# Block-sparse attention with a soft mixture of experts: the turned probabilities of a tile share one buffer, and neighbouring keys share products

## The chip, the cores and the metric

The kernel runs on one core of one Trainium2 chip. The metric is the device time of one launch in microseconds (us), the median of the runs shown.

## The reference

Four batches of eight heads, 768 positions, 64 values a head; positions are grouped into 24 blocks of 32. A query block sees its own block and the two beside it, the first and the last block (the "boundary" blocks), and three sampled blocks; the first and last query blocks see everything. The attention's output (3072 x 512) goes through a soft mixture of 8 experts with 4 slots each.

```python
mask = np.abs(blk_i - blk_j) <= 1
mask = mask | (blk_i == 0) | (blk_j == 0) | (blk_i == n_blocks - 1) | (blk_j == n_blocks - 1)
for qb in range(n_blocks):
    for kb in sampled_blocks[qb]:
        mask[qb*32:(qb+1)*32, kb*32:(kb+1)*32] = True
attn = softmax(np.where(mask, q @ k.T / 8, -1e9))
x = (attn @ v)                       # as 3072 x 512
logits = x @ phi                     # 512 x 32 slots
d = softmax(logits, axis=0); c = softmax(logits, axis=1)
slot_input = d.T @ x
slot_out[e] = np.maximum(slot_input[e] @ w1[e], 0) @ w2[e]
out = c @ slot_out
```

## The kernel before

All of the arithmetic is in float32. The kernel has three stages: attention with the logits of the mixture beside it, the experts, and the output.

In attention the 22 inner query blocks of a batch are taken in 11 *pairs*. For a pair, `stage_k` (L414) gathers for each of its two blocks the 256 keys that it sees into a buffer `kst`, eight blocks of 32: three neighbours, two boundary blocks, three sampled ones. The fixed blocks are copied by POOL (L434, L436), the sampled ones by ACT (L442) or POOL (L444). `qk` (L515) makes the scores `s`, VectorE their maxima `nm` (L530), ACT the probabilities `p` (L535), and VectorE turns them by transposes of 32 x 32 into `ptt` (L542), so that keys lie on the partitions. The 128 partitions of a turned tile are four heads of 32 keys, and there are two such sets of heads, r = 0 and 1. `stage_v` (L460) gathers the values of the sampled blocks into `vrs`.

Two neighbouring pairs make a *full tile* of four query blocks, 128 output rows; there are five in each batch, and one tile of a single pair beside the dense first and last blocks. `av_heads` multiplies the turned probabilities with the values (`v`, and `vrs` for the sampled blocks) into the PSUM tile `av`, of which there is one; all of its products stand on one line, L593 (`av_mm`). A product's stationary side is a part of `ptt`: 64 partitions (two heads, the index g) by as many columns as query rows take part, 32 for each block; its moving side is 130 columns of values. Two r passes fill a full tile. Then VectorE normalizes into `x` (L587 to L589), TensorE transposes `x` (`mxt`, L772), and four tiles form a group for the logits (`ml`), their running sums (`ms`) and `d`; there are six groups. The dense blocks have their own scores (`sd`, L684) and products (`avd`, also L593).

The order on each engine is written once, at build time, by a planner (`Plan.run`): every step is a task with the steps that it needs, a key, a cost that its author put in (2.36 for one r pass of a full tile), and the buffers that it takes from named rings (`ptt` 4, `x` 6, `s` 4, `av` 1). The planner goes through the tasks by their earliest start and lists the instructions of each engine in that order. SP's loads of the expert weights are paced by TensorE's progress, into buffers that are kept for them or that attention has given back.

The layout of `ptt` before: for each tile and r a buffer of eight slots by four query blocks by 32, the slots being the eight key blocks of each query's own list. Slots 4 and 5 hold the boundary blocks for all four query blocks. A neighbour that two blocks of one pair share stands in the same slot for both (slots 1 and 2), so their product has 64 columns; the other neighbours and the sampled ones are products of 32 columns.

Of the kernel before, what the change touches and what calls it, by code (L numbers as in the profile page):

```python
# [11 lines left out]
F32 = mybir.dt.float32  # L12
I32 = mybir.dt.int32
# [22 lines left out]


NKST, NVR, NQ = 4, 6, 4
PB, PTB, XB, XTB = 4, 4, 6, 4
SB, MB = 4, 2  # L40

LD0, LD1 = 3, 12
# [140 lines left out]
def attn_moe_kernel(ctx, tc, qT, kT, vfull, vtab, sampled, phi, w1, w2, out):  # L183
# [64 lines left out]
    ssum = const.tile([P, 1], F32, name="ssum")  # L248


    sreg = const.tile([1, NB, NR], I32, name="sreg")

    vreg = const.tile([1, NB, NR], I32, name="vreg")

    scr = pw.tile([P, DM], F32, tag="x", name="scr", bufs=XB)

# [44 lines left out]
        n = (B * (NB - 2) + n) % NVR  # L301
        vrs[n] = pst.tile([P, 2, NR, 2 * D1], F32, name=f"vrs{n}")

    nq = [0]

    def load_q(b, g, eng=None):
        q = qst[nq[0] % NQ]
# [43 lines left out]
    def evac(out, in_, eng):  # L351
        if eng in ("A", "ACT"):
            ACT.copy(out=out, in_=in_)  # L353
        else:
            DVE.tensor_copy(out=out, in_=in_)

    plan = Plan(tc, dict(s=SB, av=1, pt=MB, p=PB, ptt=PTB, kst=NKST, vrs=NVR, x=XB, xT=XTB, k=2, v=2, q=NQ,
                     ptd=1, lp=1, dT=1, d=1), free=("pt",))
    add = plan.add

    class Rec:
# [15 lines left out]
    use = []  # L377
    t_warm = add(warm, ("PE", 4.0), [], -41, acq=[("s", use)])
    use.append(t_warm)
    t_sreg = add(sreg_copy, ("DVE", 0.3), [t_idx], -39)  # L380
    t_vreg = add(lambda t: index_math(), ("DVE", 4.0), [t_sreg], -38)

# [37 lines left out]

    fresh, nst, nvs = {}, [0], [0]

    def stage_k(b, i, n, use):
        k = nst[0] % NKST
        nst[0] += 1
        st, new = kst[k], fresh.get(k) != b
        fresh[k] = b

        w, r0 = (0, 96) if i % 2 else (32, 0)

        def fixed(t):
            kv = ktile[b]
            if new:
                POOL.tensor_copy(out=st[:, :, 128:192].rearrange("p c (g s) -> p c g s", g=2),  # L434
                                 in_=kv.rearrange("p c (g s) -> p c g s", g=NB)[:, :, 0:NB:NB - 1, :])
            POOL.tensor_copy(out=st[:, :, w:w + 96], in_=kv[:, :, (i - 1) * BLK:(i + 2) * BLK])  # L436

        def sampled_(t):
            for j, o in enumerate((r0, 192, 224)):
                src = ktile[b][:, :, ds(t.vals[j] * BLK, BLK)]  # L440
                if t.eng == "ACT":
                    ACT.activation(out=st[:, :, o:o + BLK], in_=src, func=AF.Copy, scale=1.0)  # L442
                else:
                    POOL.tensor_copy(out=st[:, :, o:o + BLK], in_=src)  # L444

        f = add(fixed, ("POOL", 0.82 if new else 0.47), [t_k[b]], n - 4, acq=[("kst", use)])
        r = add(sampled_, [("ACT", 0.62), ("POOL", 0.73)], [f, t_sreg], n - 2.5,
                pre=lambda e: block_numbers(sreg, i, e, NB - 1))
        k_use[b].extend([f, r])
        use.extend([f, r])  # L450
        return st, r
# [43 lines left out]

    def plan_pair(b, g, n):
        T = tile_of(b, (g + 1) // 2)
        w = 1 if g and g % 2 == 0 else 0
        u = Rec()
        u.g = g  # L500
        kd, ku = [], []
# [20 lines left out]
            use.append(t_qk)  # L522
        u.p = [None] * 2
        if not T.turned:
            T.pt = [None] * 2
        for r in range(2):
            def top(t, r=r):
                u.nm = getattr(u, "nm", {})
                u.nm[r] = pw.tile([P, 2], F32, tag="nm", name="nm", bufs=4)
                DVE.tensor_reduce(out=u.nm[r], in_=u.s[r], axis=AX.X, op=ALU.max, negate=True)  # L530

            def exp(t, r, j):
                if j == 0:
                    u.p[r] = pw.tile([P, 2, 256], F32, tag="p", name="p", bufs=PB)
                ACT.activation(out=u.p[r][:, j, :], in_=u.s[r][:, j, :], func=AF.Exp,  # L535
                               bias=u.nm[r][:, j:j + 1], scale=1.0)


            def turn(t, r=r):
                if w == 0:  # L540
                    T.pt[r] = pw.tile([P, 8, 4, BLK], F32, tag="ptt", name="ptt", bufs=PTB)
                DVE.transpose(out=T.pt[r][:, :, 2 * w:2 * w + 2, :].rearrange("p k j q -> p j k q"),  # L542
                              in_=u.p[r].rearrange("p j (k q) -> p j k q", k=8))

            t_m = add(top, ("DVE", 0.6), [t_qk], n + 0.1 + 0.01 * r)
            p_use = []
            t_e = []
            for j in range(2):
                t_e.append(add(lambda t, r=r, j=j, exp=exp: exp(t, r, j), ("ACT", 0.37), [t_m] + t_e, n + 0.2 + 0.01 * r,
                               acq=[("p", p_use)] if j == 0 else []))  # L550
            s_use[r].append(t_e[1])
            acq = []
            if w == 0:
                T.pt_use = getattr(T, "pt_use", {})
                T.pt_use[r] = []
                acq = [("ptt", T.pt_use[r])]
            t_t = add(turn, ("DVE", 0.64), [t_e[1]] + ([T.turned[r]] if w else []), n + 0.3 + 0.01 * r, acq=acq)
            p_use.append(t_t)
            T.turned.append(t_t)
# [41 lines left out]
    def av_heads(T, rs_):  # L601

        vt, us = vtile[T.b], T.units
        one = len(us) == 1
        m = 64 * len(us)
        for n, c in enumerate((4, 5)):
            for r in rs_:
                for g, s_ in G2:
                    av_mm(T.av, 64 * r if one else 0, m, g, r, T.pt[r][s_, c, 0:m // BLK].rearrange("p j q -> p (j q)"),
                          vt[s_, :, VPOS((0, NB - 1)[n]), r, :], n == 0, False)  # L610
        for c in (1, 2):
            for w, u in enumerate(us):
                for r in rs_:
                    for g, s_ in G2:
                        av_mm(T.av, 64 * r if one else 64 * w, 64, g, r,
                              T.pt[r][s_, c, 2 * w:2 * w + 2].rearrange("p j q -> p (j q)"),
                              vt[s_, :, VPOS(2 * u.g + c), r, :], False, False)
        for n in range(NR + 1):
            for w, u in enumerate(us):
                for r in rs_:  # L620
                    for j in range(2):
                        i = 2 * u.g + 1 + j
                        for g, s_ in G2:
                            if n == 0:

                                k, c = (i - 1, 0) if j == 0 else (i + 1, 3)
                                if k in (0, NB - 1):
                                    continue
                                v_ = vt[s_, :, VPOS(k), r, :]
                            else:  # L630
                                c = ((3, 0)[j], 6, 7)[n - 1]
                                v_ = u.vst[j][s_, :, n - 1, r, :]
                            av_mm(T.av, (64 * r if one else 64 * w) + 32 * j, 32, g, r, T.pt[r][s_, c, 2 * w + j], v_,
                                  False, n == NR)

    def plan_av(T, n):
        deps = T.turned + T.staged + [t_v[T.b]]
        use, x_use = [], T.x_use
        if len(T.units) == 1:
            def both(t):  # L640
                new_av(T)
                av_heads(T, range(2))

            def out(t):
                for r in range(2):
                    av_out(T, T.av, 64 * r, 64 * r + 64, slice(r, r + 1), 0)
            t_a = add(both, ("PE", 2.45), deps, n + 0.5, acq=[("av", use)])
            T.out = [add(out, ("DVE", 1.68), [t_a], n + 0.6)]
        else:
            def heads(t, r):  # L650
                if r == 0:
                    new_av(T)
                av_heads(T, (r,))
            t_0 = add(lambda t: heads(t, 0), ("PE", 2.36), deps, n + 0.5, acq=[("av", use)])
            t_a = add(lambda t: heads(t, 1), ("PE", 2.36), [t_0], n + 0.5)
            T.out = [add(lambda t: av_out(T, T.av, 0, P), ("DVE", 1.06), [t_a], n + 0.6, acq=[("x", x_use)])]
        x_use.extend(T.out)
        use.extend(T.out)
# [106 lines left out]
    def plan_group(gi, Ts, last, final=False):  # L765
# [65 lines left out]
            PE.transpose(st.pd, st.dT, ident)  # L831

        def dout(t):
            st.d = pw.tile([P, P], F32, tag="d", name="d", bufs=1)
            evac(st.d, st.pd, "D")

        def sums(t):
# [25 lines left out]
        lp_use.extend([t_lt, t_e])  # L863
        t_dt = add(dturn, ("PE", 0.25), [t_e], k + 0.4, acq=[("pt", use[2])])
        dT_use.append(t_dt)
        t_do = add(dout, ("DVE", 0.2), [t_dt], k + 0.5, acq=[("d", d_use)])
        use[2].append(t_do)
        t_s = add(sums, ("PE", 1.1), [t_do], k + 0.6, acq=[("pt", use[3])])
        d_use.append(t_s)
# [60 lines left out]
    def c_out(g, bank, eng="A"):  # L930
        if g in (3, 4):
            cT[g] = pw.tile([P, 4, P], F32R, tag="p", name="cT", bufs=PB)
        elif g in (0, 2):
            both_ = pw.tile([P, 2, 4, P], F32R, tag="ptt", name="cT", bufs=PTB)
            cT[g], cT[{0: 1, 2: 5}[g]] = both_[:, 0], both_[:, 1]
        evac(cT[g], bank, eng)

    def plan_combine(g, n, dep=[]):
# [123 lines left out]
    for j, g in enumerate((0, 1, 2, 5)):  # L1062
# [8 lines left out]
        t_n = add(lambda t, g=g: c_rest(g), ("POOL", 0.95), [t_n], n + 0.1)  # L1071
        t_n = add(turn, ("PE", 0.62), [t_n, done[-1][1].t_av], n + 0.2, acq=[("s", b_use)])
        p_use.append(t_n)
        b_use.append(add(lambda t, g=g: c_out(g, cb[g]), ("ACT", 0.6), [t_n], n + 0.3, acq=[("ptt", [])] if g in (0, 2) else []))
    c3 = plan_combine(3, k + 1.2, [t_7])
    t_8 = add(lambda t: c_max(4), ("DVE", 0.55), [t_lst[m] for m in range(16, 20)] + [t_7], k + 1.7)
    add(lambda t: c_exp(4), ("ACT", 0.32), [t_8], k + 1.8)
# [286 lines left out]
```

## Time and profile before

| | |
|---|---|
| median of three runs | 314.02 us (312.48 to 316.74) |
| profiled execution | 318.06 us, its span 316.3 us |
| TensorE busy | 281.0 us, 89% of the span |
| VectorE, POOL, ACT busy | 214.8, 181.1, 164.7 us |
| HBM read, written | 56.19 MB, 6.29 MB |
| probability products (L593, `av`) | 1728 records with `v`, 2112 with `vrs` |

A float32 product leaves two records of TensorE (PE) in the trace, and two weight loads (PEld). In a row, "64*128 64x130" is a product with 64 partitions by 128 output rows on the stationary side and 130 moving columns on 64 partitions. Page part 2 shows TensorE near full from the first microseconds to the end of the expert stage, and the DMA engines at nine tenths or more in the last quarter of the span.

### The profile page before, as it was taken

The numbers are of one execution on the slowest core, as the hardware profiler recorded it, in microseconds if no ns is written. First come the engines' busy times: TensorE is split into PE (matmuls) and PEld (weight loads), VectorE is DVE, ScalarE is ACT, GpSimd is POOL, SyncE is SP. The second block draws the span as 40 slices with busy tenths as digits, with TensorE's granted clock in tenths as the row PEclk, the third lists the DMA queues.
The fourth block names the chain that finished last, engine by engine and source line by source line (L and its number), as shares of the span: only waits on it lengthen the run. The fifth ranks groups of instructions, "written<-read, shape, count | busy, mean of one in ns | idle before, by whom it ended". The sixth has DMA issues, their size and how long they took to land.

```text
span 316.3 us, 17629 instructions
## 1 busy us (share of the span) xinstructions
PE 281.0 (89%) x7179; PEld 193.9 (61%) x7179; DVE 214.8 (68%) x495; ACT 164.7 (52%) x505; POOL 181.1 (57%) x503
## 2 busy tenths in 40 slices
PE   7499789799997989999999999997997999999960
PEld 7148557466774656778676667864765774355540
DVE  4799766658997589789977878997597335012260
ACT  0856665853666687636757753764662140102350
POOL 2879488685954868776688885748557314000000
PEclk9999999999999999999999999998999999999996
DMA  7935777610265725034575311668688999999998
GB/s 250 398 103 173 218 204 208 165 41 3 71 184 153 206 75 146 6 87 138 138 219 139 115 55 34 167 187 222 183 226 271 367 302 370 368 412 407 393 356 288
DMA packets 34227, 63.63 MB, mean 201 GB/s; under 512 B 5601, under 2 KB 19042, under 8 KB 34146
## 3 DMA queue, kind: packets, MB, share of 16 engines
q1 hardware_dynamic: 34000, 62.37, 61.9%
q8 instruction: 57, 0.93, 1.3%
q14 instruction: 24, 0.20, 0.2%
q10 hardware_dynamic: 146, 0.13, 0.1%
HBM read 56.19 MB, written 6.29 MB: 198 GB/s over the span
## 4 chain that ended last, share of the span: by engine, by line
PE 56%; DMA 14%; DVE 9%; issue 7%; POOL 3%; ACT 3%; POOLq 3%; ACTq 2%; SPq 1%; DVEq 0%
PE av L593 24%; PE s L515 7%; DMA q<-in_qT_dram 6%; PE pf L1162 4%; PE avd L593 4%; DMA w<-in_w_dram 3%; PE sd L684 3%; PE mxt L772 3%; PE pso L1170 3%; DMA v<-in_vfull_dram 3%; POOLq L341 2%; PE ml L790 2%; DMA ktile<-in_kT_dram 2%; DVE ptt L542 2%; ACTq L341 2%
## 5 line engine op out<-in xcount | busy, mean ns | idle before, releaser
L460 POOL COPY vrs<-v 128x260 f32 x264 | 96.0, 407 | 31.9 <-PE av L593 22.3
L535 ACT ACTIVATE p<-s,nm 128x256 f32<-128x256 f32 x176 | 72.2, 476 | 15.4 <-DVE nm L530 12.9
L593 PE MATMUL av<-v,ptt 64*64 64x130 f32 (+2 forms) x1728 | 75.8, 287 | 0.4 <-issue 0.4
L542 DVE STREAM_TRANSPOSE ptt<-p 128x512 f32<-128x512 f32 x88 | 58.8, 693 | 21.2 <-ACT p L535 21.1
L593 PEld LDWEIGHTS av<-v,ptt 64*64 64x64 f32 (+2 forms) x1728 | 50.9, 133 | 27.7 <-issue 18.0
L515 PE MATMUL s<-kst,q 64*32 64x256 f32 x1408 | 53.5, 382 | 10.5 <-ACT p L535 6.0
L530 DVE TENSOR_REDUCE nm<-s 128x2 f32<-128x512 f32 x88 | 55.4, 671 | 0.5 <-PE s L515 0.3
L436 POOL COPY kst<-ktile 128x384 f32<-128x384 f32 x88 | 42.9, 509 | 14.6 <-PE s L515 12.2
L593 PE MATMUL av<-vrs,ptt 64*32 64x130 f32 x2112 | 46.5, 275 | 4.3 <-issue 4.2
L442 ACT ACTIVATE kst<-ktile 128x128 f32 x174 | 39.5, 305 | 11.3 <-PE s L515 8.3
L515 PEld LDWEIGHTS s<-kst,q 64*32 64x32 f32 x1408 | 28.9, 106 | 23.6 <-ACT p L535 9.4
L593 PEld LDWEIGHTS av<-vrs,ptt 64*32 64x32 f32 x2112 | 35.3, 105 | 7.0 <-issue 6.2
L593 PE MATMUL avd<-v,ptd 64*64 64x130 f32 x768 | 23.8, 271 | 0.7 <-DVE ptd L719 0.4
L353 ACT COPY xT<-mxt 128x512 f32<-128x512 f32 x20 | 11.7, 585 | 24.4 <-PE mxt L772 23.0
L715 ACT ACTIVATE pd<-sd,nb 128x384 f32<-128x384 f32 x32 | 16.6, 577 | 14.8 <-DVE nb L710 14.3
L593 PEld LDWEIGHTS avd<-v,ptd 64*64 64x64 f32 x768 | 22.0, 132 | 3.0 <-PE s L515 1.5
L444 POOL COPY kst<-ktile 128x128 f32 x90 | 22.7, 296 | 1.0 <-issue 0.6
L477 ACT ACTIVATE q<-q 128x256 f32<-128x256 f32 x26 | 10.8, 417 | 19.0 <-DMA q<-in_qT_dram 18.7
L479 POOL TENSOR_SCALAR q<-q 128x256 f32<-128x256 f32 x22 | 8.9, 407 | 17.3 <-DMA q<-in_qT_dram 17.3
L772 PE MATMUL mxt<-ident,x 128*128 128x128 f32 x96 | 15.8, 286 | 3.2 <-DVE x L589 3.2
L772 PEld LDWEIGHTS mxt<-ident,x 128*128 128x128 f32 x96 | 10.1, 141 | 13.7 <-DVE x L589 6.0
L587 DVE TENSOR_SCALAR rs<-av 128x8 f32<-128x8 f32 (+1 forms) x28 | 4.5, 162 | 20.6 <-PE av L593 20.4
(117 smaller groups left out, 296.8 us busy)
## 6 DMA issues: line engine op xcount, KB each, us to landing
q<-in_qT_dram SPq DMA_DIRECT2D x47, 128.0 KB, 2.7
w<-in_w_dram SPq DMA_DIRECT2D x44, 128.0 KB, 3.0
w<-in_w_dram SPq DMA_DIRECT2D x11, 512.0 KB, 9.6
out_dram<-ob SPq DMA_DIRECT2D x22, 256.0 KB, 4.3
ktile<-in_kT_dram SPq DMA_DIRECT2D x48, 96.0 KB, 2.9
w<-in_w_dram SPq DMA_DIRECT2D x18, 256.0 KB, 6.6
v<-in_w_dram SPq DMA_DIRECT2D x24, 128.0 KB, 3.4
v<-in_w_dram SPq DMA_DIRECT2D x12, 256.0 KB, 5.3
```

Of the source, the lines that this page charges most:

```text
L341: _, vals = nc.values_load_multi_w_load_instructions(t[0:1, i, :], engines=[{"ACT": E_.Activation, "POOL": E_.Pool}[eng]], min_val=0, max_ ...
L436: POOL.tensor_copy(out=st[:, :, w:w + 96], in_=kv[:, :, (i - 1) * BLK:(i + 2) * BLK])
L442: ACT.activation(out=st[:, :, o:o + BLK], in_=src, func=AF.Copy, scale=1.0)
L444: POOL.tensor_copy(out=st[:, :, o:o + BLK], in_=src)
L460: POOL.tensor_copy(out=st[:, :, j:j + 1, :], in_=vf[:, :, ds(t.vals[j], 1), :])
L515: PE.matmul(u.s[r][32 * p:32 * p + 32, j, :], lhsT=u.q[s_, p, j, :], rhs=kd[j][0][s_, p, :], start=True, stop=True)
L530: DVE.tensor_reduce(out=u.nm[r], in_=u.s[r], axis=AX.X, op=ALU.max, negate=True)
L535: ACT.activation(out=u.p[r][:, j, :], in_=u.s[r][:, j, :], func=AF.Exp, bias=u.nm[r][:, j:j + 1], scale=1.0)
L542: DVE.transpose(out=T.pt[r][:, :, 2 * w:2 * w + 2, :].rearrange("p k j q -> p j k q"), in_=u.p[r].rearrange("p j (k q) -> p j k q", k=8))
L593: PE.matmul(av[o:o + m, g, r * 2 * D1:(r + 1) * 2 * D1].rearrange("p (a d) -> p a d", a=2), lhsT=lhsT, rhs=rhs, start=start, stop=stop)
L715: ACT.activation(out=u.p[r][k], in_=u.s[r][k], func=AF.Exp, bias=u.nb[r], scale=1.0)
L772: PE.transpose(T.px[:, c, :], T.x[:, c * P:(c + 1) * P], ident)
```

## The change

The four `ptt` buffers become one, with four places of eleven slots that begin nine slots apart. Query block c of a tile (c = 0 to 3) lies c slots further than before, and the order of the keys in `kst` now depends on c, so that a key block that several query blocks of the tile see as a neighbour stands in one slot for all of them. The slots of the tile: 3 and 4 are the boundary blocks, 5 to 10 the neighbours, and the sampled blocks take what is left. Each neighbouring key block is then one product for the query blocks from `lo` to `hi`: one, two, three or four of them. For the third one, the range is widened to all four blocks, and the place of the first block, which doesn't see this key, holds zeros, which POOL writes once at the start. The boundary products stay as they were (128 columns), and so do the 24 sampled ones of a pass (32 columns). Per pass of a full tile there are 40 products for 44. For tiles of a single pair the products have the same widths as before.

To make room, `x` has five buffers for six, `d` shares the buffer of `lp`, and `sreg` and `vreg` share one. The cost of a pass in the planner becomes 2.15.

```diff
-PB, PTB, XB, XTB = 4, 4, 6, 4
+PB, PTB, XB, XTB = 4, 4, 5, 4
+PTS, PTD = 11, 9
...
+    ptt = pw.tile([P, (PTB - 1) * PTD + PTS, 4, BLK], F32, name="ptt", tag="ptt", bufs=1)
...
+    def zeros(t):
+        for r in range(PTB):
+            POOL.memset(ptt[:, PTD * r + 8, 0, :], 0.0)
...
+    SPOS = [[k for k in range(5) if k not in (3 - c, 4 - c)] for c in range(4)]
...
-        w, r0 = (0, 96) if i % 2 else (32, 0)
+        c = (i + 1) % 4
+        w, o_ = 5 * BLK, (3 - c) * BLK
...
-            T.pt = [None] * 2
+            T.pt = [ptt[:, PTD * ((nt[0] + r) % PTB):PTD * ((nt[0] + r) % PTB) + PTS] for r in range(2)]
+            nt[0] += 2
...
-                if w == 0:
-                    T.pt[r] = pw.tile([P, 8, 4, BLK], F32, tag="ptt", name="ptt", bufs=PTB)
-                DVE.transpose(out=T.pt[r][:, :, 2 * w:2 * w + 2, :].rearrange("p k j q -> p j k q"),
-                              in_=u.p[r].rearrange("p j (k q) -> p j k q", k=8))
+                a_ = T.pt[r][:, 2 * wl, 2 * wl, :].copy()
+                o = bass.AP(a_.tensor, a_.offset, [list(a_.ap[0]), [5 * BLK, 2], [4 * BLK, 8], [1, BLK]])
+                DVE.transpose(out=o, in_=u.p[r].rearrange("p j (k q) -> p j k q", k=8))
...
-        for c in (1, 2):
-            for w, u in enumerate(us):
+        for s in (1, 2, 3, 4, 0, 5):
+            k = k0 + s - 1
+            lo, hi = max(c0, (0, 0, 0, 0, 2, 3)[s]), min(4, s + 1)
+            if lo < hi and k not in (0, NB - 1):
                 for r in rs_:
                     for g, s_ in G2:
-                        av_mm(T.av, 64 * r if one else 64 * w, 64, g, r,
-                              T.pt[r][s_, c, 2 * w:2 * w + 2].rearrange("p j q -> p (j q)"),
-                              vt[s_, :, VPOS(2 * u.g + c), r, :], False, False)
+                        mm(r, g, s_, 5 + s, lo, hi, vt[s_, :, VPOS(k), r, :])
...
-            t_0 = add(lambda t: heads(t, 0), ("PE", 2.36), deps, n + 0.5, acq=[("av", use)])
+            t_0 = add(lambda t: heads(t, 0), ("PE", 2.15), deps, n + 0.5, acq=[("av", use)])
```

TensorE, the first pass of the first full tile, before (the first six of its rows: the boundary blocks, the shared neighbours, the single neighbours, and the first sampled ones; "128x130 x4" is four products with 128 output rows):

```order
L593 MATMUL av<-v_68,ptt 128x130 x4
L593 MATMUL av<-v_68,ptt 64x130 x8
L593 MATMUL av<-v_68,ptt 32x130 x8
L593 MATMUL av<-vrs_105,ptt 32x130 x2
L593 MATMUL av<-vrs_106,ptt 32x130 x2
L593 MATMUL av<-vrs_101,ptt 32x130 x2
```

The same place on TensorE with the change:

```order
L607 MATMUL av<-v_68,ptt 128x130 x4
L607 MATMUL av<-v_68,ptt 64x130 x2
L607 MATMUL av<-v_68,ptt 96x130 x2
L607 MATMUL av<-v_68,ptt 128x130 x2
L607 MATMUL av<-v_68,ptt 64x130 x2
L607 MATMUL av<-v_68,ptt 32x130 x4
L607 MATMUL av<-vrs_104,ptt 32x130 x2
```

The sixteen neighbour products in two widths became twelve in four widths, which come in the order 64, 96, 128, 64, 32. The twelve rows of sampled products behind them are as before.

TensorE between the two passes of that tile, before (`s` are the scores of another pair):

```order
L593 MATMUL av<-vrs_102,ptt 32x130 x2
L515 MATMUL s<-kst_95,q_99 32x256 x8
L515 MATMUL s<-kst_96,q_99 32x256 x8
L593 MATMUL av<-v_68,ptt 128x130 x4
L593 MATMUL av<-v_68,ptt 64x130 x8
```

And with the change:

```order
L607 MATMUL av<-vrs_105,ptt 32x130 x2
L607 MATMUL av<-vrs_100,ptt 32x130 x2
L607 MATMUL av<-vrs_101,ptt 32x130 x2
L607 MATMUL av<-v_68,ptt 128x130 x4
L607 MATMUL av<-v_68,ptt 64x130 x2
```

The second pass now follows the first at once, and the scores that stood between them come behind both.

VectorE around the same tile, before (`nm` are maxima of scores, `ptt` transposes, `rs` and `x` the normalizing of the tile):

```order
L542 STREAM_TRANSPOSE ptt<-p 128x2x8x32 x4
L530 TENSOR_REDUCE nm<-s 128x2 x2
L587 TENSOR_SCALAR rs<-av 128x8
L588 RECIPROCAL rs<-rs 128x8
L589 TENSOR_TENSOR x<-av,rs 128x512
```

And with the change:

```order
L557 STREAM_TRANSPOSE ptt<-p 128x2x8x32 x4
L601 TENSOR_SCALAR rs<-av 128x8
L602 RECIPROCAL rs<-rs 128x8
L603 TENSOR_TENSOR x<-av,rs 128x512
L543 TENSOR_REDUCE nm<-s 128x2 x4
```

The two maxima of the scores that stood between the passes moved behind the normalizing, as the scores did on TensorE. The transposes have the same shape and stand at the same place.

More of the change, by code (lines that the diff above doesn't have):

```diff
@@ L248, in attn_moe_kernel @@
     ssum = const.tile([P, 1], F32, name="ssum")
-    sreg = const.tile([1, NB, NR], I32, name="sreg")
-    vreg = const.tile([1, NB, NR], I32, name="vreg")
+    reg = const.tile([2 * BLK, NB, NR], I32, name="reg")
+    sreg, vreg = reg[0:1], reg[BLK:BLK + 1]
     scr = pw.tile([P, DM], F32, tag="x", name="scr", bufs=XB)
@@ L302, in attn_moe_kernel @@
         vrs[n] = pst.tile([P, 2, NR, 2 * D1], F32, name=f"vrs{n}")
-    nq = [0]
+    ptt = pw.tile([P, (PTB - 1) * PTD + PTS, 4, BLK], F32, name="ptt", tag="ptt", bufs=1)
+    nq, nt = [0], [0]
     def load_q(b, g, eng=None):
@@ L357, in attn_moe_kernel @@
     plan = Plan(tc, dict(s=SB, av=1, pt=MB, p=PB, ptt=PTB, kst=NKST, vrs=NVR, x=XB, xT=XTB, k=2, v=2, q=NQ,
-                     ptd=1, lp=1, dT=1, d=1), free=("pt",))
+                     ptd=1, lp=1, dT=1), free=("pt",))
     add = plan.add
@@ L379, in attn_moe_kernel @@
     use.append(t_warm)
+    def zeros(t):
+        for r in range(PTB):
+            POOL.memset(ptt[:, PTD * r + 8, 0, :], 0.0)
+    t_zero = add(zeros, ("POOL", 0.4), [], -36)
     t_sreg = add(sreg_copy, ("DVE", 0.3), [t_idx], -39)
@@ L433, in fixed @@
             if new:
-                POOL.tensor_copy(out=st[:, :, 128:192].rearrange("p c (g s) -> p c g s", g=2),
+                POOL.tensor_copy(out=st[:, :, o_:o_ + 2 * BLK].rearrange("p c (g s) -> p c g s", g=2),
                                  in_=kv.rearrange("p c (g s) -> p c g s", g=NB)[:, :, 0:NB:NB - 1, :])
@@ L438, in sampled_ @@
         def sampled_(t):
-            for j, o in enumerate((r0, 192, 224)):
+            for j, o in enumerate(BLK * k for k in SPOS[c]):
                 src = ktile[b][:, :, ds(t.vals[j] * BLK, BLK)]
@@ L497, in plan_pair @@
         T = tile_of(b, (g + 1) // 2)
-        w = 1 if g and g % 2 == 0 else 0
+        w, wl = (1 if g and g % 2 == 0 else 0), 1 - g % 2
         u = Rec()
@@ L604, in av_heads, with mm @@
         one = len(us) == 1
-        m = 64 * len(us)
-        for n, c in enumerate((4, 5)):
+        k0, c0 = 2 * us[0].g + 1 - 2 * one, 2 * one
+        def mm(r, g, s_, slot, lo, hi, v_, start=False, stop=False):
+            av_mm(T.av, 64 * r + BLK * (lo - c0) if one else BLK * lo, BLK * (hi - lo), g, r,
+                  T.pt[r][s_, slot, lo:hi].rearrange("p j q -> p (j q)"), v_, start, stop)
+        for n in range(2):
             for r in rs_:
                 for g, s_ in G2:
-                    av_mm(T.av, 64 * r if one else 0, m, g, r, T.pt[r][s_, c, 0:m // BLK].rearrange("p j q -> p (j q)"),
-                          vt[s_, :, VPOS((0, NB - 1)[n]), r, :], n == 0, False)
@@ L611, in av_heads @@
-        for c in (1, 2):
-            for w, u in enumerate(us):
+                    mm(r, g, s_, 3 + n, c0, 4, vt[s_, :, VPOS((0, NB - 1)[n]), r, :], n == 0)
+        for s in (1, 2, 3, 4, 0, 5):
+            k = k0 + s - 1
+            lo, hi = max(c0, (0, 0, 0, 0, 2, 3)[s]), min(4, s + 1)
+            if lo < hi and k not in (0, NB - 1):
                 for r in rs_:
                     for g, s_ in G2:
-                        av_mm(T.av, 64 * r if one else 64 * w, 64, g, r,
-                              T.pt[r][s_, c, 2 * w:2 * w + 2].rearrange("p j q -> p (j q)"),
-                              vt[s_, :, VPOS(2 * u.g + c), r, :], False, False)
@@ L618, in av_heads @@
-        for n in range(NR + 1):
-            for w, u in enumerate(us):
-                for r in rs_:
[L621 to L634, printed above, removed]
+                        mm(r, g, s_, 5 + s, lo, hi, vt[s_, :, VPOS(k), r, :])
@@ L636, in plan_av @@
+        for n in range(NR):
+            for c in range(c0, 4):
+                for r in rs_:
+                    for g, s_ in G2:
+                        mm(r, g, s_, SPOS[c][n] + c, c, c + 1, us[(c - c0) // 2].vst[c % 2][s_, :, n, r, :], False, n == NR - 1)
     def plan_av(T, n):
-        deps = T.turned + T.staged + [t_v[T.b]]
+        deps = T.turned + T.staged + [t_v[T.b], t_zero]
         use, x_use = [], T.x_use
@@ L653, in heads @@
                 av_heads(T, (r,))
-            t_0 = add(lambda t: heads(t, 0), ("PE", 2.36), deps, n + 0.5, acq=[("av", use)])
-            t_a = add(lambda t: heads(t, 1), ("PE", 2.36), [t_0], n + 0.5)
+            t_0 = add(lambda t: heads(t, 0), ("PE", 2.15), deps, n + 0.5, acq=[("av", use)])
+            t_a = add(lambda t: heads(t, 1), ("PE", 2.15), [t_0], n + 0.5)
             T.out = [add(lambda t: av_out(T, T.av, 0, P), ("DVE", 1.06), [t_a], n + 0.6, acq=[("x", x_use)])]
@@ L833, in dout @@
         def dout(t):
-            st.d = pw.tile([P, P], F32, tag="d", name="d", bufs=1)
+            st.d = pw.tile([P, P], F32, tag="lp", name="d", bufs=1)
             evac(st.d, st.pd, "D")
@@ L865, in plan_group @@
         dT_use.append(t_dt)
-        t_do = add(dout, ("DVE", 0.2), [t_dt], k + 0.5, acq=[("d", d_use)])
+        t_do = add(dout, ("DVE", 0.2), [t_dt], k + 0.5, acq=[("lp", d_use)])
         use[2].append(t_do)
@@ L932, in c_out @@
             cT[g] = pw.tile([P, 4, P], F32R, tag="p", name="cT", bufs=PB)
-        elif g in (0, 2):
-            both_ = pw.tile([P, 2, 4, P], F32R, tag="ptt", name="cT", bufs=PTB)
-            cT[g], cT[{0: 1, 2: 5}[g]] = both_[:, 0], both_[:, 1]
+        else:
+            if g not in cT:
+                both_ = pw.tile([P, 4, 4, P], F32R, tag="ptt", name="cT", bufs=1)
+                cT.update({h: both_[:, j] for j, h in enumerate((0, 1, 2, 5))})
         evac(cT[g], bank, eng)
@@ L1073, in attn_moe_kernel @@
         p_use.append(t_n)
-        b_use.append(add(lambda t, g=g: c_out(g, cb[g]), ("ACT", 0.6), [t_n], n + 0.3, acq=[("ptt", [])] if g in (0, 2) else []))
+        b_use.append(add(lambda t, g=g: c_out(g, cb[g]), ("ACT", 0.6), [t_n], n + 0.3))
     c3 = plan_combine(3, k + 1.2, [t_7])
```

## The prediction

> **What bounds the kernel now.** I read the page first, then the engines by stretch, then what TensorE waits for, and last one product pass in order of time. The page says that TensorE is busiest, and that the chain that ended last runs over it for more than half of the span, the probability products first:
>
> ```profile
> PE 281.0 (89%) x7179; PEld 193.9 (61%) x7179; DVE 214.8 (68%) x495; ACT 164.7 (52%) x505; POOL 181.1 (57%) x503
> PE 56%; DMA 14%; DVE 9%; issue 7%; POOL 3%; ACT 3%; POOLq 3%; ACTq 2%; SPq 1%; DVEq 0%
> L593 PE MATMUL av<-v,ptt 64*64 64x130 f32 (+2 forms) x1728 | 75.8, 287 | 0.4 <-issue 0.4
> L593 PE MATMUL av<-vrs,ptt 64*32 64x130 f32 x2112 | 46.5, 275 | 4.3 <-issue 4.2
> ```
>
> A share of busy time is a mean over unlike stages, so the stretches come next (start:end, length, then busy microseconds and instructions of PE, its weight loads, DVE, ACT and POOL, granted clock, DMA share, GB/s):
>
> ```profile
> 32.00:92.00 60.00, 54.00 (x1624) 38.31 (x1617) 44.69 (x95) 36.18 (x112) 41.52 (x117) 1.00 0.48 134
> 92.00:152.00 60.00, 55.95 (x1676) 39.90 (x1674) 49.28 (x108) 38.06 (x121) 43.39 (x122) 1.00 0.41 117
> 152.00:208.00 56.00, 53.04 (x1638) 39.38 (x1634) 47.16 (x105) 35.93 (x116) 42.02 (x118) 1.00 0.48 131
> 208.00:252.00 44.00, 40.04 (x1156) 28.63 (x1143) 30.40 (x71) 21.76 (x70) 27.06 (x74) 0.96 0.79 240
> 252.00:316.30 64.30, 52.12 (x567) 30.11 (x566) 19.05 (x57) 15.87 (x37) 4.58 (x8) 0.96 1.00 362
> ```
>
> From 32 to 252 us, the attention stage, TensorE is busy for 54.00 + 55.95 + 53.04 + 40.04 = 203 of 220 us, and VectorE, the next, for 171.5. So this stage is TensorE's, with 17 us of idle time in it. After 252 us the DMA share is 1.00: weights stream into buffers that attention held. That tail has a fixed amount to move, so what is gained or lost before 252 us shifts the end by about as much. What fills TensorE's idle time there (waiter, what it waited for, microseconds, times, longest):
>
> ```profile
> PE s L515 <- ACT p L535: 6.0, 5, 1.6
> PE av L593 <- issue: 4.6, 8, 1.8
> PE mxt L772 <- DVE x L589: 2.9, 7, 0.9
> PE s L515 <- issue: 1.4, 1, 1.4
> ```
>
> **What one pass costs.** A pass is the products of one full tile for one r: 44 before, 40 after. Each product leaves two records, so a pass has 88. The pass at 103.84 us, cut where the output width changes from 128 to 64 to 32 columns (these instructions alone: PE and weight loads):
>
> ```profile
> 103.84:104.48 0.64, 0.64 (x8) 0.52 (x8) 1.00 0.87 283
> 104.48:105.09 0.61, 0.61 (x18) 0.43 (x16) 1.00 0.75 186
> 105.09:106.19 1.10, 1.10 (x68) 0.90 (x64) 1.00 0.88 248
> sum 2.35, PE 2.35 PEld 1.86; mean PE 0.78 PEld 0.62
> ```
>
> The first stage has 8 records of 128 columns, the second 16 of 64 (18 are shown, since two of the first still run), the third 64 of 32. So 8 records take 0.64 us and 64 take 1.10 us: the time doesn't go by the count. It goes by how records fit side by side. Each stands on one half of the rows (the two g), and on a quarter, a half or all of the columns. In a **round**, everything that doesn't overlap runs at once: 2 records of 128, 4 of 64 or 8 of 32. The stages have 4, 4 and 8 rounds, 16 in all.
>
> The dense products give the price of a round, because all 192 records of a group are 64 wide, which makes 48 rounds:
>
> ```profile
> 143.28 5.79 PE L593 MATMUL avd<-v,ptd 64*64 64x130 f32 x192
> 149.01 0.33 PE L808 MATMUL lt<-ident,lp 128*128 128x128 f32 x1
> ```
>
> From its start to the next form at 149.01 are 5.73 us. With one round T and one **toll** t for beginning and leaving a form, 48T + t = 5.73 and 4T + t = 0.61, so T = 0.116 us and t = 0.145 us. The 128-wide stage leaves 0.64 - 4T = 0.175 and the 32-wide one 1.10 - 8T = 0.17 for its toll. The toll is seen on the weight loads, which otherwise run without a break:
>
> ```profile
> 103.84 1.08 PEld L593 LDWEIGHTS av<-v,ptt 64*128 64x128 f32 x24 [0.41 <-PE s L515]
> 105.09 0.18 PEld L593 LDWEIGHTS av<-v,ptt 64*32 64x32 f32 x16 [0.17 <-issue]
> 105.23 0.76 PEld L593 LDWEIGHTS av<-vrs,ptt 64*32 64x32 f32 x48
> 106.20 0.38 PEld L790 LDWEIGHTS ml<-xT,phis 128*32 128x32 f32 x16 [0.20 <-issue]
> 93.71 0.76 PEld L593 LDWEIGHTS av<-vrs,ptt 64*32 64x32 f32 x48
> 94.41 0.19 PEld L515 LDWEIGHTS s<-kst,q 64*32 64x32 f32 x2
> ```
>
> Where the form changes (64*64 to 64*32 at 105.09, to 128*32 at 106.20) the loads pause for 0.17 to 0.20 us; where another line goes on with the same 64*32 (the last two rows, of another pass: 93.71 + 0.76 reaches past 94.41) there is no pause. [...]
>
> **The change, part by part.** The boundary keys stay: 128 wide, 4 rounds, 0.64 us. The neighbours were 8 products of 64 and 8 of 32 (or 6, where a neighbour is a boundary block): 4 rounds and 2. Now they are 12 products, in the order 64, 96, 128, 64, 32, 32 columns, two (the g) of each:
> - The first key covers only the left half: 2 rounds at half use, 2T + 0.145 = 0.377 us.
> - The 96-wide and 128-wide keys can't stand beside each other: 4 rounds. A 96-wide record isn't in this trace; I take it as one of the 128 form, which is the nearest, so one toll covers both: 4T + 0.175 = 0.64 us. Its other bound is a form of its own, one toll more.
> - The fourth key covers only the right half: 0.377 us.
> - The two 32-wide keys take the outer column quarters, the 24 sampled products follow, 6 rounds on each quarter. If a free quarter runs ahead, the stage stays at 8 rounds, 1.10 us; if all four keep step, two rounds more would be 0.23 us. I take the first, because the stage before had the same 8 rounds on its fullest quarter.
>
> A pass becomes 0.64 + 0.377 + 0.64 + 0.377 + 1.10 = 3.13 us against 2.35, **0.78 us longer with four products fewer**: 4 rounds (0.46) and two tolls (0.32). Tiles of one pair get the same widths as before. Twenty full tiles, two passes each, make 40 x 0.784 = 31.4 us of TensorE time.
>
> What of it is covered? Idle time that ends on another engine's work shrinks when TensorE arrives later. Each of the five waits on ACT's exponentials (6.0 us) has a pass ahead of it, so between 5 x 0.784 = 3.9 and 6.0 us go; the 1.4 us wait behind two passes goes; of the 4.6 us inside passes ("issue": nothing shown ended them, so instructions came late) between none and all. The 2.9 us on VectorE's normalized x stay, since x itself waits for the pass. Together 5.3 to 12.0 us; I take 8. Net: 31.4 - 8 = **+23.4 us**.
>
> The other edits I cost at nothing:
> - The turned writes stay 128x512 transposes with another stride. Nearest row: 693 ns each, 58.8 us in all, so a tenth more would be 6 us, on an engine with 48 us idle.
> - One shared buffer could make a transpose wait for products of another tile. In the program order each transpose waits for ACT only, so nothing is added; a wait there would hold the rows of maxima behind it on VectorE, and with them ACT.
> - The four zero fills stand on POOL ahead of the identity that TensorE's warm-up waits for. An identity-sized fill took 0.20 us, so at most 0.8 us, and the first scores wait for their keys until 8.65 us, long after:
>
> ```profile
> 0.73 0.20 POOL masks.py:197 MEMSET ident<- 128x128 f32 x1 [0.29 <-POOLq L1350]
> 8.65 0.15 PEld L684 LDWEIGHTS sd<-ktile,q 64*32 64x32 f32 x8 [0.47 <-DMA ktile<-in_kT_dram]
> ```
>
> - Five x buffers for six: four belong to a group until its sums, one is left for the next tile. If that were one short, each of six groups could hold a pass back by about a sums step (1 us): up to 6 us more. The tile shared by d and lp serves steps that already follow each other.
> - The second pass of a tile now often follows the first at once instead of behind a score block. Scores and sampled products share the form 64*32, so the tolls don't change.
>
> **Rivals.**
> 1. *The products' count decides, faster.* Place: the product pass on TensorE. At 2.35 / 44 = 0.053 us a product, four fewer save 0.214 us, times 40 = 8.5 us: 305.5 us. It decides if a narrow product costs what a wide one does. Against it: 64 records in 1.10 us, 8 in 0.64. [...] 5%.
> 2. *No toll between forms on the array's parts*, 4 rounds only: 40 x 0.464 = 18.6, less 6 covered: 326.6 us. 9%.
> 3. *Another engine or queue had the time*: all 17 us idle and 3 us of late instructions are swallowed, 31.4 - 20 = 11.4: 325.4 us. For it: VectorE is busy at 82% from 92 to 152 us. Against it: the x waits can't be swallowed. 8%.
> 4. *Dearer forms*: 96 as its own form adds 40 x 0.16 = 6.4 (343.8), quarters in step 9.3 (346.7), one x buffer short 6 (343.4). 15%.
>
> **How the numbers follow.** The profiled execution took 318.06 us, of which 316.3 is the span; it would become 341.5. The three runs shown have a median of 314.02, 4 us lower, so the forecast for the median is 314.0 + 23.4 = 337.4 us, at 63%, itself from 333 to 341 by the bounds of what is covered. The range, 324 to 351 us, takes in rivals 2, 3 and 4 and leaves out the first and pairs of the dearer forms. Within 2% (about what these runs can tell from no change) ends at 320.3 us. Faster holds rival 1, 5%; within 2% gets 6%, from rivals 2 and 3 with more cover than I count; slower 89%.
>
> **What would show it.** In the profile after, a full pass should take about 3.1 us, with five pauses of 0.15 to 0.2 us on the weight loads where there were three, the 96-wide and 128-wide keys without a pause between them, and the last stage still near 1.10 us. The attention stage should end near 275 us, with less TensorE idle time on ACT, and the tail should be as long as now. I am wrong if a pass is shorter than 2.35 us, if the pauses are missing, or if the stage's end moves by much more than the passes explain.

## Result, and the profile after

The changed kernel took 325.23 us (median of four runs, 324.68 to 325.75), the kernel before, timed beside it, 315.38 us: a ratio of 1.031, with a 95% interval from 1.0249 to 1.0372. It is slower, as forecast, but by 9.9 us where 23.4 were forecast. The runs of a kernel fall into faster and slower ones; medians here are of all runs and ratios of the faster ones alone, so a ratio can differ by up to 1% from the quotient of the medians beside it.

The page of the changed kernel, the lines that answer to those of before (the third is a new line of part 5, the fourth the queue that brings TensorE's instructions, as its counts in the last section show):

```profile
span 324.0 us, 16990 instructions
PE 302.1 (93%) x6855; PEld 211.2 (65%) x6855; DVE 217.7 (67%) x497; ACT 164.5 (51%) x503; POOL 180.2 (56%) x507
L607 PE MATMUL av<-v,ptt 64*64 64x130 f32 (+3 forms) x1408 | 104.9, 294 | 0.1
q8 instruction: 54, 0.88, 1.1%
```

TensorE is busy for 302.1 us against 281.0, with 324 records fewer. The pass at 101.09 us, cut at the changes of form as before (these instructions alone; a count includes records of the form ahead that still run):

```profile
101.09:101.74 0.65, 0.65 (x9) 0.53 (x9) 1.00 0.72 219
101.74:102.11 0.37, 0.37 (x7) 0.19 (x5) 1.00 0.42 136
102.11:102.73 0.62, 0.62 (x11) 0.50 (x9) 1.00 0.50 115
102.73:103.10 0.37, 0.37 (x7) 0.20 (x5) 1.00 0.80 242
103.10:104.20 1.10, 1.10 (x58) 0.89 (x56) 1.00 0.92 253
sum 3.11, PE 3.11 PEld 2.30; mean PE 0.62 PEld 0.46
```

The forecast said 0.64, 0.377, 0.64, 0.377 and 1.10, together 3.13. All 40 passes are alike: the last record of a pass starts 2.91 to 2.94 us after its first. The weight loads of the same pass:

```profile
101.08 0.84 PEld L607 LDWEIGHTS av<-v,ptt 64*128 64x128 f32 x12 [0.17 <-issue]
102.11 0.81 PEld L607 LDWEIGHTS av<-v,ptt 64*96 64x96 f32 x12 [0.18 <-issue]
103.09 0.14 PEld L607 LDWEIGHTS av<-v,ptt 64*32 64x32 f32 x6 [0.17 <-issue]
104.19 0.38 PEld L800 LDWEIGHTS ml<-xT,phis 128*32 128x32 f32 x16 [0.20 <-issue]
```

Between the 96-wide and the 128-wide keys there is no pause: row two holds both, and the 64-wide loads behind them too, after a pause of 0.12 us that is too short to begin a row. The attention stage and the tail, before and after:

```profile
32.00:252.00 220.00, 203.05 (x6074) 146.21 (x6067) 171.53 (x376) 131.93 (x416) 153.99 (x429) 0.99 0.52 150
...
32.00:259.30 227.30, 223.10 (x5757) 162.41 (x5756) 174.80 (x378) 131.95 (x415) 153.50 (x430) 1.00 0.49 145
259.30:324.00 64.70, 52.39 (x567) 30.20 (x567) 19.06 (x57) 15.96 (x37) 4.55 (x8) 0.95 1.00 362
```

TensorE's idle time in attention fell from 17 us to 4.2, and the tail is 64.7 us for 64.3. What it still waits for from 31 to 260 us:

```profile
PE mxt L782 <- DVE x L603: 2.1, 3, 1.3
PE avd L607 <- DVE ptd L729: 0.8, 2, 0.4
PE ms L850 <- ACT kst L453: 0.6, 1, 0.6
PE s L527 <- ACT p L548: 0.5, 2, 0.3
```

The waits on ACT are down from 6.0 us to 0.5, and the breaks inside passes ("issue", 4.6 us before) are gone. From the first pass to the end of the last, the two traced executions differ by 6.8 us (by 7.7 over the whole span, where the medians differ by 9.9; the one before ran 2.7 us over its median). TensorE's records say where the 6.8 come from: 40 passes longer by 0.755 us, +30.2; passes no longer broken or slowed, -8.4; scores that run through without stopping, -5.5; idle time outside passes, -8.1; the rest, -1.4.

### The profile page after: what moved, and what is told of

It is laid out like the page before. It is cut to its first block, busy times and chain, and to the rows that moved or that the text cites. A ratio compares the mean times of both kernels' runs of the same rounds, so it can differ in the third digit from the quotient of the medians.

```text
span 324.0 us, 16990 instructions
## 1 busy us (share of the span) xinstructions
PE 302.1 (93%) x6855; PEld 211.2 (65%) x6855; DVE 217.7 (67%) x497; ACT 164.5 (51%) x503; POOL 180.2 (56%) x507
## 4 chain that ended last, share of the span: by engine, by line
PE 69%; DVE 13%; DMA 9%; ACT 4%; issue 2%; SPq 1%; ACTq 0%; DVEq 0%
PE av L607 35%; PE s L527 8%; PE avd L607 5%; PE pf L1173 4%; PE mxt L782 3%; DMA w<-in_w_dram 3%; DMA q<-in_qT_dram 3%; PE pso L1181 3%; DVE x L603 3%; PE sd L694 3%; DVE ptd L729 2%; ACT p L548 2%; DMA ktile<-in_kT_dram 2%; DVE nm L712 2%; PE ml L800 2%; PE ms L850 2%
## 5 line engine op out<-in xcount | busy, mean ns | idle before, releaser
L607 PE MATMUL av<-v,ptt 64*64 64x130 f32 (+3 forms) x1408 | 104.9, 294 | 0.1
L607 PEld LDWEIGHTS av<-v,ptt 64*64 64x64 f32 (+3 forms) x1408 | 67.9, 148 | 38.9 <-issue 23.4
L527 PE MATMUL s<-kst,q 64*32 64x256 f32 x1408 | 47.6, 379 | 3.4 <-POOL kst L455 2.8
L607 PE MATMUL av<-vrs,ptt 64*32 64x130 f32 x2112 | 50.4, 277 | 0.0
L607 PEld LDWEIGHTS av<-vrs,ptt 64*32 64x32 f32 x2112 | 38.4, 105 | 0.0
L527 PEld LDWEIGHTS s<-kst,q 64*32 64x32 f32 x1408 | 29.8, 106 | 11.6 <-POOL kst L455 3.4
L725 ACT ACTIVATE pd<-sd,nb 128x384 f32<-128x384 f32 x32 | 16.7, 578 | 21.5 <-DVE nb L720 20.9
L356 ACT COPY xT<-mxt 128x512 f32<-128x512 f32 x18 | 10.5, 586 | 23.3 <-PE mxt L782 23.2
L712 DVE TENSOR_REDUCE nm<-sd 128x1 f32<-128x384 f32 x32 | 16.4, 545 | 4.2 <-PE sd L694 4.1
L782 PEld LDWEIGHTS mxt<-ident,x 128*128 128x128 f32 x96 | 10.1, 140 | 12.7 <-DVE x L603 5.2
L694 PE MATMUL sd<-ktile,q 64*32 64x384 f32 x256 | 17.4, 529 | 0.9 <-ACT p L548 0.6
L603 DVE TENSOR_TENSOR x<-av,rs 128x512 f32<-128x512 f32 (+1 forms) x28 | 17.2, 614 | 1.0
```

The lines of the kernel that those rows point to most:

```text
L527: PE.matmul(u.s[r][32 * p:32 * p + 32, j, :], lhsT=u.q[s_, p, j, :], rhs=kd[j][0][s_, p, :], start=True, stop=True)
L603: DVE.tensor_tensor(out=x, in0=a[:, :, :, 0:D], in1=rs[lo:hi].unsqueeze(3).to_broadcast([hi - lo, 2, 2 * n, D]), op=ALU.mult)
L607: PE.matmul(av[o:o + m, g, r * 2 * D1:(r + 1) * 2 * D1].rearrange("p (a d) -> p a d", a=2), lhsT=lhsT, rhs=rhs, start=start, stop=stop)
L694: PE.matmul(u.s[r][k][32 * p:32 * p + 32, :], lhsT=T.dq.q[s_, p, j, :], rhs=kt[s_, p, 384 * k:384 * (k + 1)], start=True, stop=True)
L712: DVE.tensor_reduce(out=u.nm[r][:, k:k + 1], in_=u.s[r][k], axis=AX.X, op=ALU.max, negate=True)
```

## Experiments

Three things could have made the 21.5 us that disappeared between 31.4 us of longer passes and 9.9 us of result. Theory A: the length itself (other engines and the instruction supply get more time). Theory B: the planner's other order, which its cost of 2.15 brings about. Theory C: the smaller number of products, because instructions come in pages (fetches of 16 KB, 57 before and 54 with the change). Each ratio is to the kernel before, timed beside the run, with its 95% interval.

**Length alone, old order.** The kernel before, its pass stretched to 3.06 us by the order of its products (the edit in words):

```diff
-  boundaries (128), shared neighbours (64), single neighbours (32), sampled (32)
+  first boundary (128), one shared (64), single (32), second boundary (128), the other three shared (64), sampled (32)
```

> The kernel before, its layout, its 44 products a pass and its order between steps, but inside a full tile's pass the forms follow each other as 128, 64, 32, 128, 64, 32: three more changes of form and two rounds at half use. By rounds and tolls a pass takes 3.09 us for 2.35, 0.74 x 40 = 29.6 us more TensorE time, about what the change adds. Theory A (the longer pass itself covers waits and late instructions): most is swallowed as in the changed kernel, 322 to 328 us. Theory B (the changed order between steps took the waits away): here the order is the old one, so it arrives but for the 8 us that the prediction covered: 335 to 345 us.

331.33 against 318.61 us, 1.049 [1.036, 1.062]. Of 40 x 0.71 = 28.4 us in passes, by the trace's own records, 0.049 x 315.4 = 15.5 us arrived by the ratio and 12.7 by the medians: between the ranges of A and B, and more than in the changed kernel. In the trace the attention stage grew by 11.4 us. What covers the rest is seen in its waits (31 to 264 us), against 6.0 and 4.6 us before:

```profile
PE s L515 <- ACT p L535: 1.2, 2, 1.0
PE av L593 <- issue: 0.9, 1, 0.9
```

**Order alone, old length.** One number, which puts TensorE's steps into the changed kernel's order:

```diff
-            t_0 = add(lambda t: heads(t, 0), ("PE", 2.36), deps, n + 0.5, acq=[("av", use)])
-            t_a = add(lambda t: heads(t, 1), ("PE", 2.36), [t_0], n + 0.5)
+            t_0 = add(lambda t: heads(t, 0), ("PE", 2.15), deps, n + 0.5, acq=[("av", use)])
+            t_a = add(lambda t: heads(t, 1), ("PE", 2.15), [t_0], n + 0.5)
```

> The kernel before with one number changed: the planner's cost of a pass, 2.15 for 2.36. TensorE's steps then stand in the changed kernel's order (both passes of a tile mostly back to back), with the old layout, 44 products and 2.35 us a pass. Theory B (the order is worth something by itself): 3 to 6 us less than before, ratio 0.98 to 0.99. If the order is worth nothing: 0.995 to 1.005.

314.02 against 316.35 us, 0.987 [0.981, 0.994]: the order is worth 1.3% by itself, about 4 us (0.7% by the medians). Which part of the order does that isn't shown. "Mostly back to back" was too much said: by the traces the two passes of a tile follow each other at once in 10 of 20 tiles in the old order and in 11 in the new one, though partly in other tiles.

**Both.** The stretched kernel with that same edit:

> The old layout and 44 products with the pass stretched to 3.09 us by three more changes of form, as in the earlier run, and the planner's cost at 2.15, so that the steps stand in the changed kernel's order. Length and order together are then what the change has, and only the number of products differs. If these two make up the result: ratio 1.02 to 1.04, as the changed kernel, and 1 to 3% below the stretched kernel in the old order (1.049). If the order is worth nothing: 1.045 to 1.055.

325.81 against 316.35 us, 1.035 [1.026, 1.043]. Length and order together give the changed kernel's ratio within its interval, with the old layout and 44 products. The order takes off about the same here, 1.049 to 1.035, though these two were timed on different chips and their intervals overlap.

**The true cost in the planner of the changed kernel** (the first of the two lines that change).

```diff
-            t_0 = add(lambda t: heads(t, 0), ("PE", 2.15), deps, n + 0.5, acq=[("av", use)])
+            t_0 = add(lambda t: heads(t, 0), ("PE", 3.11), deps, n + 0.5, acq=[("av", use)])
```

> The changed kernel with the cost that its pass really has in the planner, 3.11 for 2.15: scores stand between the two passes of some tiles. At this length TensorE hardly waits for anybody (4.2 us in the changed kernel), so the order should matter little: ratio to before 1.025 to 1.04. If the back to back order is what saves it: 1.04 to 1.06.

328.94 against 316.35 us, 1.043 [1.032, 1.054]. I expected no difference; it points the other way, to the order again, though the interval overlaps the changed kernel's, so that it isn't shown that the honest cost made a worse order.

**The changed kernel with the old split of the neighbours** (the new loop in words).

```diff
-        for s in (1, 2, 3, 4, 0, 5):
+        # 64 columns: keys 1, 3, 2, 4; then 32 columns: keys 0, 2, 3, 5
```

> The changed kernel, its buffer, its order between steps, five x buffers, but with the neighbours split as before into 8 products of 64 columns and 8 of 32 in a pass: 44 products, 16 rounds, three tolls, 2.35 us a pass, 31 us less TensorE time than the change. Theory A: the waits come back, as long as in the kernel before, 312 to 318 us. Theory B: the order without the waits keeps its gain, 298 to 306 us. If layout or x buffers cost something of their own: above 318.

313.99 against 318.61 us, 0.989 [0.985, 0.994]: the same as order alone in the old layout (0.987). So the shared buffer, its strides, the zero fills and the five x buffers cost nothing that shows, and what the change lost, it lost in the widths of its products.

**The number of products.** First, more of them in less array time, the kernel before with its 64-wide products cut in two (lines shortened):

```diff
+                    for j in range(2):
-                        av_mm(T.av, 64 * w, 64, g, r, T.pt[r][s_, c, 2 * w:2 * w + 2] ...
+                        av_mm(T.av, 64 * w + 32 * j, 32, g, r, T.pt[r][s_, c, 2 * w + j] ...
```

> The kernel before with its eight 64-wide products of a pass split into sixteen of 32: 52 products, 16 rounds as before, but only two forms and two tolls. By rounds and tolls 2.19 us a pass, 6.4 us less TensorE time in all. Theory A: part turns into waits, 309 to 315 us. Rival C (instructions come late by their number, some 1300 more of them): the pass breaks off more often, 315 to 322 us.

325.01 against 318.61 us, 1.021 [1.008, 1.033]: slower, with a shorter pass. An unbroken pass took 2.19 us, as the rounds say, but 17 of the 40 were broken (by the spacing of their records longer than the rest by over 0.05 us), and lost 17 us together. Its waits, and its instruction queue (62 fetches, 57 before):

```profile
PE av L593 <- issue: 11.3, 13, 2.4
PE s L515 <- ACT p L535: 3.5, 2, 2.1
...
q8 instruction: 62, 1.02, 1.4%
```

Then fewer at the same rounds:

```diff
-                                if k in (0, NB - 1):
+                                if k in (0, NB - 1) or (j == 1 and not one):
```

> The kernel before, its layout and order, with four of the eight 32-wide neighbour products of a pass left out (those of each pair's second block, so that part of the attention is missing): 40 products as in the change, but the same 16 rounds and three tolls, since the fullest column quarter keeps its eight rounds: 2.35 us a pass by rounds and tolls. Theory C (TensorE gets its instructions in pages of 256, 64 products, and can't have one oftener than every 3.8 to 4 us, some 0.06 us a product; before, 44 products in 2.35 us outrun that): 4 x 40 x 0.06 = up to 9.6 us less, ratio to before 0.97 to 0.985. Theory A (only the pass's length counts): ratio 0.995 to 1.005.

312.57 against 316.09 us, 0.985 [0.975, 0.994], at the upper end of what C gives; 4 passes of 40 were broken where 12 were before, and two of the 4 only ran at a lower granted clock (0.58 from 36 to 40 us, 0.57 from 214 to 218). Theory A, which gave no change, has not the whole truth: at 2.35 us a pass, four products are worth 1.5% (1.1% by the medians).

And four more that fill free array time, in two kernels with longer passes:

```diff
+            for lo in (1, 2):
+                for g, s_ in G2:
+                    av_mm(T.av, BLK * lo, BLK, g, r, T.pt[r][s_, 8, 0], vt[s_, :, VPOS(0), r, :], False, False)
```

> The 40 products with the widest keys first, 2.58 us a pass, and four products of zeros more in a pass, on the two column quarters that have two rounds free: 44 products, the same rounds and tolls, the same result. Theory C: 44 in 2.58 us is again faster than pages come, so pauses return at every page: 4 to 9 us over the kernel without them, ratio to before 0.99 to 1.01. Theory A: no change from 0.98.

> The changed kernel with the same four products of zeros more in a pass, on the two column quarters that are free: 44 products in 3.11 us, 0.07 us a product. Theory C: slower than pages come, so nothing pauses and nothing changes: ratio to before 1.025 to 1.04, as the changed kernel. If a product had a cost of its own, 4 x 40 x 0.05 = 8 us more, 1.05 to 1.06.

At 2.58 us a pass: 313.32 against 316.09 us, 0.987 [0.978, 0.995], where the kernel without them, timed on another chip, had 0.9795 (the next experiment). The difference is smaller than C gave and lies within the intervals, but the broken passes are back: 7 of 40 where there was one, and

```profile
PE av L607 <- issue: 2.8, 3, 1.7
```

At 3.11 us: 327.81 against 316.09 us, 1.035 [1.026, 1.045]: no change from 1.031 that shows, though one pass of the 40, late in the stage, broke for 0.9 us. So the products on free column quarters cost TensorE nothing that shows by themselves (1.035 for 1.031 at 3.11 us a pass); at 2.58 us instructions were late in some passes, by the waits on "issue" (2.8 us in three).

**The 40 products in a better order.** Wide ones first, so that they share the boundaries' form, and the two 64-wide keys beside each other:

```diff
-        for s in (1, 2, 3, 4, 0, 5):
+        for s in (2, 3, 1, 4, 0, 5):
```

> The changed kernel with its 40 products in another order: the 96 and 128 columns wide keys directly behind the boundary blocks, then the two of 64 beside each other, then the 32s. 18 rounds and three tolls: 2.58 us a pass, 0.53 x 40 = 21 us less TensorE time than the change. Theory A: only about a third of it shows, 315 to 321 us. Theory B: nearly all shows, 304 to 309 us.

310.26 against 318.61 us, 0.9795 [0.972, 0.987]: faster than both kernels, outside what A gave. Its pass is 2.58 us by the trace, 0.23 us longer than before, and still it wins: 39 of 40 passes run unbroken, and the order is the better one. No wait on "issue" is listed for its passes and scores. Its span and its largest waits there:

```profile
span 308.0 us, 16990 instructions
PE s L527 <- ACT p L548: 2.4, 2, 1.3
PE mxt L782 <- DVE x L603: 2.4, 4, 1.3
```

How much hangs on the planner's order is seen with two other costs of the pass (2.58, its true length, and 1.90).

> The 40 products with the widest keys first, with the pass's cost in the planner at 2.58 instead of 2.15: the planner then puts scores between the two passes of a tile, as in the kernel before. Theory B (the order has a part of the gain): slower than with 2.15, ratio to before 0.985 to 1.0. Theory A or C: the order costs nothing, 0.975 to 0.985.

> The 40 products with the widest keys first, 2.58 us a pass, with the planner's cost of a pass at 1.90: nearly the order that 2.15 gives. If that kernel's gain is sound: ratio to before 0.97 to 0.99 again. If its gain was an accident of one order: 0.99 to 1.0.

With 2.58: 315.10 against 316.09 us, 0.997 [0.993, 1.002]. With 1.90: 312.27 against 316.35 us, 0.990 [0.985, 0.996]. The same products spread over 1.8% by the order alone. These ratios come from different chips. The gain of the reordered products is 1 to 2% over before with the orders that 2.15 and 1.90 give, and none that shows with the order that a true cost gives.

## Why the prediction was right and wrong

- **The pass: right.** Rounds and tolls gave 3.13 us; it took 3.11, with five pauses on the weight loads for three (0.12 to 0.20 us), and the tail stayed as long as it was. They gave 2.58 and 2.19 for two other arrangements, which took 2.58 and 2.19, and 3.09 for the stretched one, which took 3.06. The 96-wide record shared the 128 form (no pause between them), and the free column quarters ran ahead (the last stage took 1.10 us): both open choices were taken right.
- **The edits at nothing: right, but for one.** The kernel with the change's layout and the old split (0.989) stands where the order alone stands (0.987), so neither the buffer nor five x buffers cost what rival 4 feared. One reading was loose, without harm: the first scores start at 7.16 us; 8.65 us is a later wait.
- **Wrong: the term "what of it is covered", 8 us of at most 12.** It was 21.5, so the attention stage ended at 259.3 us and not near 275. Three things were missed; they overlap, since the order acts through the same waits and breaks.
  - *Late instructions.* I counted the breaks that the list of waits shows, 4.6 us, as the most that could go. But TensorE counts as busy for a record's own 0.27 us after it starts (a mean of 275 ns for the sampled products before), so that a short break doesn't show as idle at all and a long one only in part. By the spacing of records, 12 of the 40 passes before were longer than the rest, together by 8.4 us more than after (one of them, 1.1 us, by a lower granted clock, 0.66 from 220 to 224 us). The trace had this, but I took one unbroken pass for all 40 and didn't add up the others.
  - *Waits on ACT.* The bounds were 3.9 to 6.0 us; 5.5 went, within them. But scores that had stopped between their records, which no wait shows, gave another 5.5 us. The slowest of them stand where scores waited for ACT; what held up each of the others isn't shown.
  - *The order.* I wrote that scores and passes in another order leave the tolls alone, which is true, and costed it at nothing. It was worth 1.3%, 4 us, with old passes, and about as much with stretched ones.
- **Two slips in the sums** changed little: the bounds of cover give 333 to 340 us, not 341, and one pair of the dearer forms (96 and the x buffer, 349.8 us) lies inside the range that was to leave pairs out. That the time lies inside the range at all, 1.2 us above its lower end, is owed to the rivals it took in, and not to the forecast's own bounds.
- **Rival 1 (the number of products decides), refuted as put.** 40 products gave no gain at 3.11 us, since four more on free quarters cost nothing that shows. But its number (2.7%) was half right at the old length, by a mechanism that the prediction had only as "instructions came late": 1.5% for four products.
- **Rival 3 (others had the time, 325.4 us) came out nearest**, and was given 8%. That it met the time within 0.2 us is luck in part: it let all 17 us of idle time go, where 12.8 went, and the rest came from broken passes and scores that it didn't count. It had the cause half: late instructions and ACT, and besides them the order. Its objection, that waits for x can't be swallowed, holds in the main: 2.1 us of 2.9 are left.
- **Rivals 2 and 4 fell**: the pauses on the weight loads are there (0.12 to 0.20 us), 96 and 128 columns have none between them, and the last stage took 1.10 us.

## What to carry over

Price products that share TensorE as these were priced, by rounds (0.116 us each, by the rows before) and changes of form (0.145 to 0.175 us each) and not by their number, and put products of one form behind each other (the 40 products took 2.58 us in the better order, for 3.11). Then read the spread of a repeated stage over all its instances before taking a single clean one as its cost: what makes the others longer can be slack that a longer stage will swallow (8.4 us here). And where a planner writes the order, a change to one of its costs is a change of its own, to be timed alone.

## What the runs showed of the hardware that I had not expected

TensorE's instructions arrived in fetches of one size (pages), and some passes waited for them. The instruction queue brought 0.93 MB in 57 fetches before, 16 KB each; 57 times 256 is 14592, and TensorE has 14545 records, its waits for semaphores included (54 times 256, 13824, for 13898 records with the change). The first fetches start when it has begun 239, 516, 736 and 1051 records. Counted so, the breaks inside passes fall at records number 2753, 5313, 8642, 9153 and 12993 before, each 193 or 194 above a multiple of 256, and so do those of the other longer passes but the one at the lower clock. With 52 products all 17 broken passes break there.

Eight breaks of the kernel before end 2.3 to 3.4 us after the fetch that precedes them begins, each time 1.35 to 1.55 us after that fetch's own duration (1.19 us and a break that ends at 2.55; 1.91 and 3.35), and in six of them the next fetch starts 1.1 to 2.0 us later (3.2 and 4.0 in the others). By these counts a page holds 256 records, 64 float32 products of four records each. From these times I estimate that a page that is used up in less than about 3.9 us, 0.06 us a product, runs dry: 52 products in 2.19 us and 44 in 2.35 do often, 40 in 2.35 and 44 in 2.58 (0.059 us a product) in two and five passes, 40 in 2.58 and 44 in 3.06 or 3.11 in at most one, and 40 in 3.11 in none. Nor is that a least distance between fetches, as theory C had it with 3.8 to 4 us: the closest two before start 3.3 us apart (138.86 and 142.18 us). One such break held TensorE for 1.8 us (the longest wait of L593 on "issue"), and the passes before lost some 7 us in all.
